# A speech joint's backward pass: the rows of two gradients taken by transposing DMAs, from sets written in a row by VectorE

## The chip, the cores and the metric

The kernel runs on one core of a Trainium2 chip. The metric is the device time of one execution in microseconds; before, three runs gave a median of 848.4 us (845.08 to 851.57). The profile is of one execution that took 843.12 us.

## What is computed

A sequence `x` of 2 x 16000 frames of 256 goes through two convolutions of three taps with a tanh-approximated gelu and a stride of 2 after each (16000 to 8000 to 4000 frames). The result `f` (projected to `fe`) is joined with 8 label vectors `ge`, and the kernel returns the joint's output and the gradients of all seven inputs for a given `grad_out`. All in bfloat16.

```python
def _fwd_reference(x, w1, w2, g, w_f, w_g, w_o):
    ...
    h = _gelu(h)[:, ::2, :]          # h: conv of x with w1, 3 taps
    ...
    f = _gelu(f)[:, ::2, :]          # f: conv of h with w2, 3 taps
    fe = jnp.einsum("btd,de->bte", f, w_f)
    ge = jnp.einsum("bud,de->bue", g, w_g)
    j = jnp.tanh(fe[:, :, None, :] + ge[:, None, :, :])
    return jnp.einsum("btud,dv->btuv", j, w_o)

def reference(x, w1, w2, g, w_f, w_g, w_o, grad_out):
    ...
    _out, _vjp = jax.vjp(_f, x, w1, w2, g, w_f, w_g, w_o)
    return (_out, *_vjp(grad_out))
```

## The kernel before, in words

Time is counted in quarter frames (one column of the kernel is one frame of `f`, four of `x`). The 2 x 4000 columns with a gap of 16 between them are cut into 16 stages of 512 columns (the last has 336; stage 7 holds the end of one batch and the start of the next, and its transfers are split). Channels lie on the partitions, 256 of them as two halves (`kt`), and time runs along the free axis.

In the loop over stages `n`, stage `n` does the joint of its own columns, the forward convolutions of stage `n+1`, and the backward of stage `n-1` below the joint. It has four steps (`up`), each for two of the eight labels. The joint is the main list, 12 units a step: the products with `WOT` (L623), the tanh gradient `NGZ` on VectorE (L627), its sum over the labels on GpSimd (L646, the last of which writes `NGFE`, bf16), the output's products (L690), their eviction on ScalarE (L692), and the gradient of `w_o` (L729). `weave` takes after each main unit 0.92 units on the average of a second list, the fill, which is a chain written out by hand:

- `conv` of stage `n+1` (L320) and `d1` (L424, the gradient through `w_f`, makes `GF`);
- `alternate(rows, d5)`: `row_units` turns `NGFE`, and the sets of `HT` and `GF`, into rows (time on the partitions) by TensorE transposes (L460), evicted by VectorE (`NGFE`) or ScalarE (L462); `d5_units` (L447) multiplies with `W2T` and VectorE writes the product with the gelu's derivative as `GH` (L450), the gradient at the first convolution's output, for even and odd frames (`par` 0 and 1);
- `gwf_units` (L506, gradient of `w_f`, from `FR` and the rows of `NGFE`) and `gw2_units` (L524, gradient of `w2`);
- `ghr_units`: the rows of `GH`, in four interleaved sets (columns k, k+4, k+8, ...), by 16 transposes on TensorE and two evictions on VectorE; between them `conv2` of stage `n+1` (L355);
- `e_units`: blocks of the gradient of `x` (L580, from `GH`), each evicted (L583) and stored by GpSimd (L241), and after each of the first three blocks one tap of the gradient of `w1` (`gw1`, L593, from the rows of `GH` and of `x`). `fe` of stage `n+1` (L379) lies among them.

Operations of an engine run in the order in which they are issued. SyncE's queue takes all transposing loads and the `grad_out` rows: `GOT` (L172, `grad_out` with channels on partitions), `XC` (L164, `x` of stage `n+2`, one a step at the end of each step in the program), `GO` (L198), `FR` (L469, rows of `f`, read in the next stage) and `JR` (L658, rows of the tanh). GpSimd's queue takes the rows of `x` (`XR`, L209) and the stores. In a regular stage SyncE issues: JR JR GOT GO XC GOT XC XC XC JR JR GOT GO GOT FR FR JR JR GO GOT GOT JR JR GO GOT GOT.

Of the kernel before, what the change touches and what calls it, by code (L numbers as in the profile page):

```python
# [13 lines left out]
BF16 = mybir.dt.bfloat16  # L14
# [18 lines left out]
def kernel(  # L33
# [76 lines left out]
    accp = pool("accp", 1)  # L110
    gfp = pool("gfp", 2)
    ghp = pool("ghp", 2)
    rowp = pool("rowp", 6)
    xrp = pool("xrp", 1)
    gxp = pool("gxp", 2)
    jtp = pool("jtp", 7)
# [313 lines left out]
    def d5_units(n):  # L430
        st = S[n]
        c0, W = geom(n)
        N = W + 1 if n == G - 1 else W
        GF, G1 = st["GF"], st["G1"]
        GH = ghp.tile([P, 2, KT, CW + 4], BF16, name="GH")
        st["GH"] = GH
        if n == 0:
            nc.gpsimd.memset(GH[:, 0, :, 1:2], 0.0)
        else:
            nc.gpsimd.tensor_copy(out=GH[:, 0, :, 1:2], in_=S[n - 1]["GH"][:, 0, :, CW + 1:CW + 2])  # L440
        for par, taps in ((0, ((1, 0),)), (1, ((2, -1), (0, 0)))):
            for mt in range(KT):
                ps = ps_f32()
                k, last = 0, len(taps) * KT - 1
                for (i, sh) in taps:
                    for kt in range(KT):
                        nc.tensor.matmul(ps[:, :N], lhsT=W2T[:, i, kt, mt * P:(mt + 1) * P],  # L447
                                         rhs=GF[:, kt, 2 + sh:2 + sh + N], start=(k == 0), stop=(k == last))
                        k += 1
                gh = nc.vector.tensor_tensor(out=GH[:, par, mt, 2:2 + N], in0=ps[:, :N],  # L450
                                             in1=G1[:, par, mt, 2 - par:2 - par + N], op=ALU.mult)
                while held:
                    tc.add_manual_dep(held.pop().ins, gh.ins.name, NOSYNC, reason="held")
                yield

    def transposes(srcs, dsts, evict=None):
# [4 lines left out]
        for dst, M, j0, j1 in dsts:  # L461
            (evict or nc.vector.tensor_copy)(out=dst, in_=ps[:M, j0:j1, :])  # L462

    def load_fr(n):
        W = geom(n)[1]
        FR = frp.tile([P, KT, 4, P], BF16, name="FR")
        nb = len(blocks(W))
        for kt in range(KT):
            nc.sync.dma_start_transpose(out=FR[:, kt, 0:nb, :], in_=S[n]["FT"][:, kt, 0:nb * P])  # L469
        S[n]["FR"] = FR  # L470

    def row_units(n):
        c0, W = geom(n)
        st = S[n]
        HT, GF, FT, NG = st["HT"], st["GF"], st["FT"], st["NGFE"]
        bl = blocks(W)
        FR = st["FR"]
        t = rowp.tile([P, 8, P], BF16, name="rows")
        st["NR"] = t
        srcs = [(NG[:, kt, o:o + M], 2 * j + kt, M) for j, (o, M) in enumerate(bl) for kt in range(KT)]  # L480
        dsts = [(t[:M, 2 * j:2 * j + 2, :], M, 2 * j, 2 * j + 2) for j, (o, M) in enumerate(bl)]
        if W == CW:
            dsts = [(t[:], P, 0, 8)]
        transposes(srcs, dsts)
        yield
# [12 lines left out]

    def gwf_units(n):
        W = geom(n)[1]  # L500
        FR, t = S[n]["FR"], S[n]["NR"]
        bl = blocks(W)
        ps = ps_f32()
        for k, (o, M) in enumerate(bl):
            for dt in range(KT):
                nc.tensor.matmul(ps[:, dt * D:(dt + 1) * D], lhsT=FR[:M, dt, k, :],  # L506
                                 rhs=t[:M, 2 * k:2 * k + 2, :].rearrange("p k d -> p (k d)"),
                                 start=(k == 0 and dt == 0), stop=(k == len(bl) - 1 and dt == KT - 1))
        flush("F", ACCF[:], ps[:])
        first_flush["F"] = False  # L510
        yield
# [27 lines left out]
    def back_sets(n):  # L539

        return [(k, M + 1 if n == G - 1 and k == 0 else M) for k, M in sets(n)]

    def ghr_units(n):
        st = S[n]
        s = nsets(n)
        GH = st["GH"]
        bl = back_sets(n)
        GR = st["GR"] = []
        for g0 in range(0, len(bl), 2):
            t = rowp.tile([P, 8, P], BF16, name="rows")  # L550
            srcs, dsts = [], []
            for j, (k, M) in enumerate(bl[g0:g0 + 2]):
                for par in range(2):
                    for kt in range(KT):
                        srcs.append((GH[:, par, kt, 2 + k:3 + k + s * (M - 1):s], 4 * j + 2 * par + kt, M))
                dsts.append((t[:M, 4 * j:4 * j + 4, :], M, 4 * j, 4 * j + 4))
                GR.append((t, 4 * j))
            if all(M == P for _, M in bl[g0:g0 + 2]):
                dsts = [(t[:, :, :], P, 0, 8)]
            transposes(srcs, dsts)  # L560
            yield

    def e_units(n):
        st = S[n]
        s = nsets(n)
        GH, GR, XR = st["GH"], st["GR"], st["XR"]
        bl = back_sets(n)

        def gx_block(k, M):
            t = gxp.tile([P, 4, D], BF16, name="GX")  # L570
            combos = (((0, 1, 0), (2, 0, -1)), ((1, 1, 0),), ((2, 1, 0), (0, 0, 0)), ((1, 0, 0),))
            for cp in range(2):
                ps = ps_f32()
                for cj in range(2):
                    cc = combos[2 * cp + cj]
                    j, last = 0, len(cc) * KT - 1
                    for (i, par, sh) in cc:
                        for kt in range(KT):
                            o = 2 + k + sh
                            nc.tensor.matmul(ps[:M, cj * D:(cj + 1) * D], lhsT=GH[:, par, kt, o:o + s * (M - 1) + 1:s],  # L580
                                             rhs=W1T[:, i, kt, :], start=(j == 0), stop=(j == last))
                            j += 1
                nc.scalar.copy(out=t[:M, 2 * cp:2 * cp + 2, :], in_=ps[:M, :])  # L583
                yield
            store_gx(n, k, t)

        def gw1(i):
            ps = ps_f32()
            for j, (k, M) in enumerate(bl):
                t, g = GR[j]  # L590
                for dt in range(KT):
                    for par in range(2):
                        nc.tensor.matmul(ps[:, dt * D:(dt + 1) * D],  # L593
                                         lhsT=XR[:M, 4 * k + i + 2 * (1 - par), dt * P:(dt + 1) * P],
                                         rhs=t[:M, g + 2 * par:g + 2 * par + 2, :].rearrange("p k d -> p (k d)"),
                                         start=(j == 0 and dt == 0 and par == 0),
                                         stop=(j == len(bl) - 1 and dt == KT - 1 and par == 1))
            flush("1", ACC1[:, i, :], ps[:])
# [225 lines left out]
    for n in range(G):  # L824
# [75 lines left out]
    for b in range(B):  # L900
        gg = ps_f32()
        for kt in range(KT):
            nc.tensor.matmul(gg[:U, 0:D], lhsT=NGGEb[:, b, kt, :], rhs=WGT[:, kt, :], start=(kt == 0), stop=(kt == KT - 1))
        gg_sb = gxp.tile([U, D], BF16, name="gg_sb")
        nc.scalar.activation(out=gg_sb[:], in_=gg[:U, 0:D], func=ACT.Copy, scale=-1.0)
        nc.sync.dma_start(out=out_4[b], in_=gg_sb[:])
# [3 lines left out]
        ngR = gxp.tile([U, KT, P], BF16, name="ngR")  # L910
        nc.vector.tensor_copy(out=ngR[:], in_=tr[:U, 0:KT, :])
# [37 lines left out]
```

## Time and profile before

| | |
|---|---|
| median of three runs | 848.4 us (845.08 to 851.57) |
| the profiled execution | 843.12 us |
| its span in the profile | 841.4 us |
| mean granted TensorE clock | 0.994 |
| mean DMA traffic | 187.21 MB, 223 GB/s |
| length of a stage | 50.7 to 51.2 us, 53.0 for stage 8 |

The first part of the page gives each engine's busy time, its share of the span and the instructions; the second cuts the span in 40 slices, each digit the busy share in tenths. The groups give, for a line and its tiles, the count, then the busy time and the mean ns of one, then the idle time ahead of them and what ended it. In a timeline, columns are the start, the length, the engine, the line and the tiles, and the number of instructions; of SyncE's queue (SPq) the length is the time that the issue took, not the transfer.

Some more rows: how the pieces of the queue land, from issue to landing, as the page's medians.

```profile
GOT<-in_grad_out_dram SPq DMA_TRANSPOSE x136, 5.7
JR<-JT SPq DMA_TRANSPOSE x128, 4.8
```

### The profile page before, as it was taken

How to read it: one execution, taken by the hardware profiler on the slowest of the kernel's cores; microseconds unless marked ns; L12 is line 12 of the kernel's file. 1: busy time of each engine (PE TensorE's matmuls, PEld its weight loads, DVE VectorE, ACT ScalarE, POOL GpSimd, SP SyncE). 2: the span in 40 equal slices, each digit the busy share in tenths (PEclk: the TensorE clock that was granted, in tenths of full speed). 3: DMA queues.
4: the chain of work that ended last, by engine and by line, in shares of the span. 5: the costliest groups of instructions: out<-in, count | busy, mean ns of one | idle time of the engine just before them, and what ended most of it. 6: DMA issues, size and time to landing. Idle time of an engine off the chain costs nothing.

```text
span 841.4 us, 17055 instructions
## 1 busy us (share of the span) xinstructions
PE 812.8 (97%) x6396; PEld 598.2 (71%) x6396; DVE 620.3 (74%) x1217; ACT 678.4 (81%) x1080; POOL 394.6 (47%) x423
## 2 busy tenths in 40 slices
PE   7969999999999999999999999999999999999997
PEld 3546677767768677676766777677686776878796
DVE  4896696876778767697866968768687676967644
ACT  3889998796978969699796987969789696987744
POOL 1154544444534535444486644445345354445661
PEclk9999999999999999999999999999999999999999
DMA  9988999999999999999999999999999999999954
GB/s 188 194 198 182 212 229 233 216 251 235 225 221 259 226 229 245 243 222 183 224 255 210 233 233 228 251 210 265 238 237 264 210 227 231 220 210 228 243 157 135
DMA packets 398515, 187.21 MB, mean 223 GB/s; under 512 B 346464, under 2 KB 382200, under 8 KB 398432
## 3 DMA queue, kind: packets, MB, share of 16 engines
q1 hardware_dynamic: 378112, 119.00, 77.9%
q0 software_dynamic: 20320, 67.12, 27.5%
q8 instruction: 50, 0.82, 0.4%
q14 instruction: 33, 0.27, 0.1%
HBM read 51.38 MB, written 50.34 MB: 121 GB/s over the span
## 4 chain that ended last, share of the span: by engine, by line
PE 43%; ACT 41%; DVE 6%; issue 5%; DMA 4%; POOL 0%; SPq 0%; ACTq 0%; POOLq 0%; DVEq 0%
ACT JT L396 12%; PE ps L593 7%; ACT OUT L692 6%; ACT JSQ L617 6%; PE GWO_ps L729 6%; PE ps L580 6%; PE ps L690 6%; ACT rows L462 5%; PE ps L355 5%; PE ps L524 4%; PE ps L623 4%; ACT g_s L260 3%; ACT g_x L323 3%; PE pst L460 2%; ACT GX L583 2%
## 5 line engine op out<-in xcount | busy, mean ns | idle before, releaser
L646 POOL TENSOR_TENSOR ACCN<-ACCN,NGZ 128x1024 f32<-128x1024 f32 (+1 forms) x80 | 168.7, 2109 | 69.1 <-DVE NGZ L627 68.0
L627 DVE SCALAR_TENSOR_TENSOR NGZ<-JSQ,ps 128x512 bf16<-128x512 bf16 (+3 forms) x272 | 167.5, 640 | 43.2 <-PE ps L623 39.9
L692 ACT CAST OUT<-ps 128x512 bf16<-128x512 f32 (+1 forms) x252 | 148.4, 600 | 58.4 <-PE ps L690 58.2
L396 ACT ACTIVATE JT<-FE,GE 128x512 bf16<-128x512 f32 (+3 forms) x272 | 182.3, 711 | 4.0 <-PE ps L623 1.9
L617 ACT ACTIVATE JSQ<-JT 128x1024 bf16<-128x1024 bf16 (+1 forms) x128 | 135.8, 1064 | 25.6 <-DVE NGZ L627 25.6
L729 PE MATMUL GWO_ps<-GO,JR 128*128 128x256 bf16 (+1 forms) x1008 | 148.6, 273 | 2.1 <-DVE JR L462 2.1
L690 PE MATMUL ps<-WO,JT 128*128 128x256 bf16 (+1 forms) x1008 | 148.7, 274 | 0.3 <-ACT rows L462 0.3
L717 POOL DMA_DIRECT2D out_dram<-OUT x76 | 55.8, 735 | 184.4 <-ACT OUT L692 171.5
L623 PE MATMUL ps<-GOT,WOT 128*128 128x512 bf16 (+1 forms) x512 | 139.2, 376 | 0.8 <-DVE rows L462 0.8
L260 DVE SCALAR_TENSOR_TENSOR g_s<-g_sq,g_x 128x1024 bf16<-128x1024 bf16 (+2 forms) x49 | 81.2, 1657 | 50.1 <-ACT g_sq L260 50.1
L729 PEld LDWEIGHTS <-JR 128*128 128x128 bf16 (+1 forms) x1008 | 96.9, 98 | 28.6 <-DVE JR L462 2.4
L690 PEld LDWEIGHTS <-JT 128*128 128x128 bf16 (+1 forms) x1008 | 97.9, 98 | 22.1 <-issue 1.6
L580 PE MATMUL ps<-W1T,GH 128*128 128x256 bf16 (+2 forms) x756 | 100.4, 273 | 0.0
L408 DVE TENSOR_TENSOR ACC<-ACC,ps 128x512 f32<-128x512 f32 x90 | 61.5, 684 | 44.5 <-PE ps L524 32.8
L580 PEld LDWEIGHTS <-GH 128*128 128x128 bf16 (+2 forms) x756 | 83.5, 116 | 13.0
L320 PE MATMUL ps<-XC,W 128*128 128x512 bf16 (+1 forms) x384 | 91.3, 375 | 1.1 <-DMA XC<-in_x_dram 1.1
L593 PE MATMUL ps<-rows,XR 128*128 128x256 bf16 (+1 forms) x756 | 90.4, 273 | 0.0
L593 PEld LDWEIGHTS <-XR 128*128 128x128 bf16 (+1 forms) x756 | 74.0, 98 | 11.6
L583 ACT CAST GX<-ps 128x512 bf16<-128x512 f32 (+2 forms) x126 | 72.2, 587 | 10.5 <-DMA out_dram<-GX 4.1
L241 POOL DMA_DIRECT2D out_dram<-GX x67 | 36.7, 548 | 82.1 <-ACT GX L583 75.0
L623 PEld LDWEIGHTS <-WOT 128*128 128x128 bf16 x512 | 48.5, 98 | 33.6 <-issue 2.3
L320 PEld LDWEIGHTS <-W 128*128 128x128 bf16 x384 | 37.4, 98 | 38.5 <-issue 1.4
(131 smaller groups left out, 1214.2 us busy)
## 6 DMA issues: line engine op xcount, KB each, us to landing
GO<-in_grad_out_dram SPq DMA_DIRECT2D x56, 512.0 KB, 5.3
out_dram<-OUT POOLq DMA_DIRECT2D x56, 512.0 KB, 5.5
out_dram<-GX POOLq DMA_DIRECT2D x55, 256.0 KB, 4.3
XR<-in_x_dram POOLq DMA_DIRECT2D x39, 256.0 KB, 6.3
XR<-in_x_dram POOLq DMA_DIRECT2D x13, 320.0 KB, 6.2
GOT<-in_grad_out_dram SPq DMA_TRANSPOSE x136, 5.7
JR<-JT SPq DMA_TRANSPOSE x128, 4.8
GO<-in_grad_out_dram SPq DMA_DIRECT2D x4, 384.0 KB, 5.0
```

The lines of the kernel that those rows point to most:

```text
L260: later.popleft()()
L320: nc.tensor.matmul(ps[:, :W], lhsT=W1[:, i, kt, mt * P:(mt + 1) * P], rhs=st["X", c][:, kt, 16 + sh:16 + sh + W], start=(k == 0), stop=(k ...
L396: nc.scalar.activation(out=JT[:, mt, lo:hi], in_=S[n]["FE"][:, mt, lo:hi], func=ACT.Tanh, bias=GE[:, b, mt, u:u + 1], scale=1.0)
L580: nc.tensor.matmul(ps[:M, cj * D:(cj + 1) * D], lhsT=GH[:, par, kt, o:o + s * (M - 1) + 1:s], rhs=W1T[:, i, kt, :], start=(j == 0), stop=( ...
L593: nc.tensor.matmul(ps[:, dt * D:(dt + 1) * D], lhsT=XR[:M, 4 * k + i + 2 * (1 - par), dt * P:(dt + 1) * P], rhs=t[:M, g + 2 * par:g + 2 * ...
L617: nc.scalar.activation(out=JSQ[:, :, :W], in_=JT[:, :, :W], func=ACT.Square)
L623: nc.tensor.matmul(ps[:, :W], lhsT=WOT[:, kt, mt * P:(mt + 1) * P], rhs=GOT[:, kt, :W], start=(kt == 0), stop=(kt == KT - 1))
L627: nc.vector.scalar_tensor_tensor(out=NGZ[:, mt, lo:hi], in0=JSQ[:, mt, lo:hi], scalar=1.0, in1=ps[:, lo:hi], op0=ALU.subtract, op1=ALU.mul ...
L646: st["last"] = nc.gpsimd.tensor_tensor(out=out, in0=in0, in1=st["NGZ", u][:, :, :W], op=ALU.add)
L690: nc.tensor.matmul(ps[:M, j * V:(j + 1) * V], lhsT=st["JT", u][:, kt, o:o + M], rhs=WO[:, kt, :], start=(kt == 0), stop=(kt == KT - 1))
L692: nc.scalar.copy(out=OUT[:M, k, :], in_=ps[:M, :])
L729: nc.tensor.matmul(GWO_ps[:, dt, :], lhsT=JR[:M, j, dt, k, :], rhs=GO[:M, k, j * V:(j + 1) * V], start=(n_gwo[0] == 0), stop=(n_gwo[0] == ...
```

## The change

The rows of `NGFE` (now `NR`) and of `GH` (now `GR`) come from transposing DMAs on SyncE's queue in all stages but the last; the transposes and evictions for them are gone there (the last stage keeps them).

- `GH` is split in two tiles, `GH0` and `GH1` (for the two `par`). VectorE writes each as four sets of 128 one after the other (the sets in reverse), reading the product in PSUM and the gelu's derivative `G1` at a step of four elements, so that a set is contiguous and one DMA turns 128-column blocks of it. The weights read from `GH` for the gradient of `x` are contiguous then.
- `load_gr` issues for each stage `GR0` as two halves (by `kt`) and `GR1` as one DMA, in the place of the fill where the rows and `d5` are done; they take no fill unit. `load_nr` issues `NR` of stage `n-1` at the start of stage `n`. `FR` becomes one DMA in place of two.
- In SyncE's queue a regular stage becomes: NR JR JR GOT GO GOT XC XC XC XC GR0 JR JR GOT GO GR0 GOT GR1 FR JR JR GO GOT GOT JR JR GO GOT GOT.
- The list of the fill: `ghr` before `gwf` and `gw2`, without the two units that it had; `rows` has one unit less (the `NGFE` rows).
- Pools: `rowp` has 4 buffers in place of 6, `NR` one and `GR` two of their own. Two small tiles of the tail move to `rowp`.

```diff
-    rowp = pool("rowp", 6)
+    rowp = pool("rowp", 4)
+    nrp = pool("nrp", 1)
+    grp = pool("grp", 2)
...
+        turned = n < G - 1
+        GH0 = ghp.tile([P, KT, CW + 4], BF16, name="GH0")
+        GH1 = ghp.tile([P, KT, CW], BF16, name="GH1")
+        st["GH"] = GH = (GH0[:, :, 2:CW + 4], GH1)
+        st["GHB"] = GH0[:, :, 1:CW + 4]
...
-                gh = nc.vector.tensor_tensor(out=GH[:, par, mt, 2:2 + N], in0=ps[:, :N],
-                                             in1=G1[:, par, mt, 2 - par:2 - par + N], op=ALU.mult)
+                out, in0, in1 = GH[par][:, mt, :N], ps[:, :N], G1[:, par, mt, 2 - par:2 - par + N]
+                if turned:
+                    out = out.rearrange("p (k m) -> p k m", k=4)
+                    in0, in1 = (bass.AP(tensor=a.tensor, offset=a.offset + 3, ap=[list(a.ap[0]), [-1, 4], [4, P]]) for a in (in0, in1))
+                gh = nc.vector.tensor_tensor(out=out, in0=in0, in1=in1, op=ALU.mult)
...
+    def load_rows(pool_, name, src, W):
+        t = pool_.tile([P, KT, 4, P], BF16, name=name)
+        if W == CW:
+            nc.sync.dma_start_transpose(out=t[:].rearrange("p k a d -> p (k a) d"), in_=src.rearrange("p k w -> p (k w)"))
+        else:
+            nb = len(blocks(W))
+            for kt in range(KT):
+                nc.sync.dma_start_transpose(out=t[:, kt, 0:nb, :], in_=src[:, kt, 0:nb * P])
+        return t
...
     def load_fr(n):
-        for kt in range(KT):
-            nc.sync.dma_start_transpose(out=FR[:, kt, 0:nb, :], in_=S[n]["FT"][:, kt, 0:nb * P])
-        S[n]["FR"] = FR
+        S[n]["FR"] = load_rows(frp, "FR", S[n]["FT"][:], geom(n)[1])
+
+    def load_nr(n):
+        S[n]["NR"] = load_rows(nrp, "NR", S[n]["NGFE"][:], geom(n)[1])
...
+    def load_gr(src, par):
+        if par:
+            return load_rows(grp, "GR", src[:], CW)
+        t = grp.tile([P, KT, 4, P], BF16, name="GR")
+        for kt in range(KT):
+            nc.sync.dma_start_transpose(out=t[:, kt], in_=src[:, kt, :CW])
+        return t
...
+        if n < G - 1:
+            ts = [load_gr(GH[par], par) for par in range(2)]
+            GR += [[t[:, :, 3 - k, :] for t in ts] for k in range(4)]
+            return
...
             parts += [islice(conv, 2), islice(d1, 1), islice(conv, 1), d1, conv, alternate(rows, d5_units(n - 1)),
-                      gwf_units(n - 1), gw2_units(n - 1), islice(ghr, 1), islice(conv2, 1), ghr, conv2, islice(e, 6)]
+                      ghr, gwf_units(n - 1), gw2_units(n - 1), conv2, islice(e, 6)]
...
+            if back and up == 0:
+                load_nr(n - 1)
```

More of the change, by code (lines that the diff above doesn't have):

```diff
@@ L434, in d5_units @@
         GF, G1 = st["GF"], st["G1"]
-        GH = ghp.tile([P, 2, KT, CW + 4], BF16, name="GH")
-        st["GH"] = GH
+        turned = n < G - 1
[3 more added lines that the diff above has]
+        st["GHB"] = GH0[:, :, 1:CW + 4]
         if n == 0:
-            nc.gpsimd.memset(GH[:, 0, :, 1:2], 0.0)
+            nc.gpsimd.memset(GH0[:, :, 1:2], 0.0)
         else:
-            nc.gpsimd.tensor_copy(out=GH[:, 0, :, 1:2], in_=S[n - 1]["GH"][:, 0, :, CW + 1:CW + 2])
+            nc.gpsimd.tensor_copy(out=GH0[:, :, 1:2], in_=S[n - 1]["GHB"][:, :, P:P + 1])
         for par, taps in ((0, ((1, 0),)), (1, ((2, -1), (0, 0)))):
@@ L462, in transposes @@
             (evict or nc.vector.tensor_copy)(out=dst, in_=ps[:M, j0:j1, :])
-    def load_fr(n):
-        W = geom(n)[1]
-        FR = frp.tile([P, KT, 4, P], BF16, name="FR")
-        nb = len(blocks(W))
-        for kt in range(KT):
-            nc.sync.dma_start_transpose(out=FR[:, kt, 0:nb, :], in_=S[n]["FT"][:, kt, 0:nb * P])
-        S[n]["FR"] = FR
+    def load_rows(pool_, name, src, W):
[7 more added lines that the diff above has]
+        return t
+    def load_fr(n):
+        S[n]["FR"] = load_rows(frp, "FR", S[n]["FT"][:], geom(n)[1])
+    def load_nr(n):
+        S[n]["NR"] = load_rows(nrp, "NR", S[n]["NGFE"][:], geom(n)[1])
     def row_units(n):
@@ L477, in row_units @@
         FR = st["FR"]
[L478 to L485, printed above, removed]
+        if "NR" not in st:
+            t = nrp.tile([P, KT, 4, P], BF16, name="NR")
+            st["NR"] = t
+            ps = ps_bf()
+            for j, (o, M) in enumerate(bl):
+                for kt in range(KT):
+                    nc.tensor.transpose(out=ps[:M, 4 * kt + j, :], in_=NG[:, kt, o:o + M], identity=ident[:])
+            for j, (o, M) in enumerate(bl):
+                nc.vector.tensor_copy(out=t[:M, :, j, :], in_=ps[:M, j:j + 5:4, :])
+            yield
         st["HG"] = []
@@ L506, in gwf_units @@
                 nc.tensor.matmul(ps[:, dt * D:(dt + 1) * D], lhsT=FR[:M, dt, k, :],
-                                 rhs=t[:M, 2 * k:2 * k + 2, :].rearrange("p k d -> p (k d)"),
+                                 rhs=t[:M, :, k, :],
                                  start=(k == 0 and dt == 0), stop=(k == len(bl) - 1 and dt == KT - 1))
@@ L541, in back_sets @@
         return [(k, M + 1 if n == G - 1 and k == 0 else M) for k, M in sets(n)]
+    def load_gr(src, par):
+        if par:
+            return load_rows(grp, "GR", src[:], CW)
+        t = grp.tile([P, KT, 4, P], BF16, name="GR")
+        for kt in range(KT):
+            nc.sync.dma_start_transpose(out=t[:, kt], in_=src[:, kt, :CW])
+        return t
     def ghr_units(n):
@@ L548, in ghr_units @@
         GR = st["GR"] = []
+        if n < G - 1:
+            ts = [load_gr(GH[par], par) for par in range(2)]
+            GR += [[t[:, :, 3 - k, :] for t in ts] for k in range(4)]
+            return
         for g0 in range(0, len(bl), 2):
-            t = rowp.tile([P, 8, P], BF16, name="rows")
+            t = grp.tile([P, KT, 4, P], BF16, name="GR")[:].rearrange("p k a d -> p (k a) d")
             srcs, dsts = [], []
@@ L554, in ghr_units @@
                     for kt in range(KT):
-                        srcs.append((GH[:, par, kt, 2 + k:3 + k + s * (M - 1):s], 4 * j + 2 * par + kt, M))
+                        srcs.append((GH[par][:, kt, k:k + s * (M - 1) + 1:s], 4 * j + 2 * par + kt, M))
                 dsts.append((t[:M, 4 * j:4 * j + 4, :], M, 4 * j, 4 * j + 4))
-                GR.append((t, 4 * j))
+                GR.append([t[:M, 4 * j + 2 * par:4 * j + 2 * par + 2, :] for par in range(2)])
             if all(M == P for _, M in bl[g0:g0 + 2]):
@@ L565, in e_units @@
         s = nsets(n)
-        GH, GR, XR = st["GH"], st["GR"], st["XR"]
+        GH, GHB, GR, XR = st["GH"], st["GHB"], st["GR"], st["XR"]
         bl = back_sets(n)
@@ L578, in gx_block @@
                         for kt in range(KT):
-                            o = 2 + k + sh
-                            nc.tensor.matmul(ps[:M, cj * D:(cj + 1) * D], lhsT=GH[:, par, kt, o:o + s * (M - 1) + 1:s],
+                            if k + sh < 0:
+                                gh = GHB[:, kt, 0:s * (M - 1) + 1:s] if n == G - 1 else GHB[:, kt, 0:M]
+                            elif n == G - 1:
+                                gh = GH[par][:, kt, k + sh:k + sh + s * (M - 1) + 1:s]
+                            else:
+                                gh = GH[par][:, kt, (3 - k - sh) * P:(3 - k - sh) * P + M]
+                            nc.tensor.matmul(ps[:M, cj * D:(cj + 1) * D], lhsT=gh,
                                              rhs=W1T[:, i, kt, :], start=(j == 0), stop=(j == last))
@@ L589, in gw1 @@
             for j, (k, M) in enumerate(bl):
-                t, g = GR[j]
                 for dt in range(KT):
@@ L594, in gw1 @@
                                          lhsT=XR[:M, 4 * k + i + 2 * (1 - par), dt * P:(dt + 1) * P],
-                                         rhs=t[:M, g + 2 * par:g + 2 * par + 2, :].rearrange("p k d -> p (k d)"),
+                                         rhs=GR[j][par],
                                          start=(j == 0 and dt == 0 and par == 0),
@@ L903 @@
             nc.tensor.matmul(gg[:U, 0:D], lhsT=NGGEb[:, b, kt, :], rhs=WGT[:, kt, :], start=(kt == 0), stop=(kt == KT - 1))
-        gg_sb = gxp.tile([U, D], BF16, name="gg_sb")
-        nc.scalar.activation(out=gg_sb[:], in_=gg[:U, 0:D], func=ACT.Copy, scale=-1.0)
-        nc.sync.dma_start(out=out_4[b], in_=gg_sb[:])
+        gg_sb = rowp.tile([P, 8, P], BF16, name="rows")[:U, 0:2, :].rearrange("u a b -> u (a b)")
+        nc.scalar.activation(out=gg_sb, in_=gg[:U, 0:D], func=ACT.Copy, scale=-1.0)
+        nc.sync.dma_start(out=out_4[b], in_=gg_sb)
         tr = ps_bf()
@@ L909 @@
             nc.tensor.transpose(out=tr[:U, kt, :], in_=NGGEb[:, b, kt, :], identity=ident[:])
-        ngR = gxp.tile([U, KT, P], BF16, name="ngR")
-        nc.vector.tensor_copy(out=ngR[:], in_=tr[:U, 0:KT, :])
+        ngR = rowp.tile([P, 8, P], BF16, name="rows")[:U, 0:KT, :]
+        nc.vector.tensor_copy(out=ngR, in_=tr[:U, 0:KT, :])
         for dt in range(KT):
```

## The prediction

> **What bounds the kernel now.** I read the busy shares first, then the slices, the queues, and for one regular stage TensorE beside SyncE's queue.
>
> ```profile
> PE 812.8 (97%) x6396; PEld 598.2 (71%) x6396; DVE 620.3 (74%) x1217; ACT 678.4 (81%) x1080; POOL 394.6 (47%) x423
> PE   7969999999999999999999999999999999999997
> DMA  9988999999999999999999999999999999999954
> q1 hardware_dynamic: 378112, 119.00, 77.9%
> q0 software_dynamic: 20320, 67.12, 27.5%
> ```
>
> TensorE is busy 97% of the span and sets the end; the chain of waits ends in its products or in their ACT evictions. But the DMA row is as full: q1 carries what SyncE issues, 119 MB, nearly all transposes in small packets; q0 what GpSimd issues. So there are two resources at their end, and the change moves work from the one to the other.
>
> The work to be removed, in the groups of instructions by form:
>
> ```profile
> L450 DVE TENSOR_TENSOR GH<-ps,G 128x512 bf16<-128x512 f32 x60 | 40.2, 684 | 2.4 <-PE ps L447 2.2
> L462 DVE COPY rows<-pst 128x1024 bf16<-128x1024 bf16 x45 | 31.0, 688 | 29.0 <-PE pst L460 29.0
> L460 PE MATMUL pst<-ident,GH 128*128 128x128 bf16 x240 | 18.3, 219 | 0.0
> L460 PE MATMUL pst<-ident,NGFE 128*128 128x128 bf16 x124 | 9.5, 219 | 0.0
> ```
>
> TensorE in stage 3 (start 172.3, counted from the stage's first L623 product), its first read of the GH rows being the L593 line, +32.5 us:
>
> ```profile
> 197.39 0.61 PE L460 MATMUL pst<-ident,GH 128*128 128x128 bf16 x8
> ...
> 199.58 0.61 PE L460 MATMUL pst<-ident,GH 128*128 128x128 bf16 x8
> ...
> 204.80 1.91 PE L593 MATMUL ps<-rows,XR 128*128 128x256 bf16 x16
> ```
>
> SyncE's queue in the same stage:
>
> ```profile
> 172.57 3.23 SPq L658 DMA_TRANSPOSE JR<-JT  x2
> 175.90 2.99 SPq L172 DMA_TRANSPOSE GOT<-in_grad_out_dram  x1
> 178.94 0.57 SPq L198 DMA_DIRECT2D GO<-in_grad_out_dram  x1
> 179.61 3.70 SPq L164 DMA_TRANSPOSE XC<-in_x_dram  x1
> 183.40 1.86 SPq L172 DMA_TRANSPOSE GOT<-in_grad_out_dram  x1
> 185.35 6.20 SPq L164 DMA_TRANSPOSE XC<-in_x_dram  x3
> 191.66 4.89 SPq L658 DMA_TRANSPOSE JR<-JT  x2
> 196.64 1.28 SPq L172 DMA_TRANSPOSE GOT<-in_grad_out_dram  x1
> 197.97 0.57 SPq L198 DMA_DIRECT2D GO<-in_grad_out_dram  x1
> 198.64 1.95 SPq L172 DMA_TRANSPOSE GOT<-in_grad_out_dram  x1
> 200.69 3.37 SPq L469 DMA_TRANSPOSE FR<-FT  x2
> ```
>
> From 172.6 to 204.1 there is no gap in this queue. Each transfer starts when the one before has been issued, not when its data are ready: FR, whose source is long written, starts at +28.4. This is the row that decides: the GR loads are queued right ahead of it.
>
> **The change part by part.** All sums are against the profiled execution, 843.1 us (span 841.4 and 1.7 around it), which is 5.3 under the median 848.4; the times move with it.
>
> 1. Removed from TensorE: 8 NGFE and 16 GH transposes in a stage, 15 stages. Eight in a row take 0.61 us with the last at 0.219, so one is (0.61 - 0.219)/7 = 0.056 us and a stage's 24 are 1.34 us, 20.1 us in all. TensorE being full, this is gain if nothing else is late: a stage of 50.8 us would take some 49.3.
>
> 2. Removed from DVE: three evictions in a stage, 3 x 0.688 = 2.06 us. DVE is 74% busy and off the path; nothing by itself.
>
> 3. GH read at a step of four and written in a row. No row has this read. Bounds: nothing, and the 1657 ns for 1024 columns of DVE's gelu products, 1.62 ns a column where L450 has 684/512 = 1.34, that is 829 ns, +0.15 us, four times a stage 0.6 us. I take 0.6: DVE has 2.06 us to spare from part 2, and GH is finished at +19.6, long before SyncE's queue comes to it. Cover gone, 0.6 us a stage.
>
> 4. FR by one DMA in place of two halves: the issue mean of JR, the same shape, is 1.73 us, two halves at the FR median of 1.42 are 2.84. 1.1 us less on the queue, but behind the GR loads, so GR has nothing of it. The gx weight loads from GH become contiguous (114 to 98 ns); weight loads overlap products, nothing. The gg_sb and ngR buffers are in the tail and short: nothing.
>
> 5. Added on SyncE: NR, at the head of the stage; GR0 in two halves; GR1. In the new order ten DMAs go before GR0's first half, GR1 is the 18th of the stage, and FR, two JR, GO and two GOT follow it. The NR issue waits for the summed gradient NGFE, which POOL finishes at +0.2, and holds all of the queue until then; in stage 3 the queue's first DMA started at +0.27 anyhow: nothing, up to 0.3. NR is read by gwf (L506 at 191.1, +18.8), lands at about +0.2 + 4.8, so it has ten us and more to spare. The first gw1 product, which waited for a DVE eviction, waits for GR1's landing instead.
>
> 6. When GR1 lands. FR began in stages 1 to 13 between 24.7 (stage 1, with nothing carried over) and 37.2 (stage 7, which holds the end of one batch and the start of the next, and has split transfers). Without stages 7 to 10, which carry that along, the median is 28.0. A stage that waits lets the queue drain, so I take 26.5, between 24.7 and 28.0. Ahead come NR (1.73, the JR mean) and GR0 (two halves, 2 x 1.42): +4.6. Issue to landing 4.8, the JR median on the page (FR's whole has 5.6). GR1 lands at 26.5 + 4.6 + 4.8 = +35.9. Bounds: 24.7 + 3.6 + 3.6 = 31.9 and 28.4 + 5.2 + 7.2 = 40.8, with three issues at 1.2 us (the FR minimum) or at JR's mean, and landings of 3.6 and 7.2, the ends of what FR took in stages 1 to 5.
>
> 7. When gw1 wants it. GH rows lie three fill units and their transposes earlier in the list of before; with those gone, the products that stand ahead of the first L593 sum to 2.2 us less than in before, so it comes at 32.5 - 2.2 = +30.3; I take +30.0. The wait is 35.9 - 30.0 = 5.9 us (bounds 1.9 and 10.8). TensorE takes its work in order, so the joint's products queue behind it, then ACT and DVE, and nothing covers it. What follows gw1 in the stage is 19.1 us of products, so the stage is 35.9 + 19.1 = 55.0 us.
>
> 8. A wait of that size also lowers TensorE's clock. In before it happens once, in stage 0 after three gaps between 52.4 and 62.0 of 1.6, 2.1 and 1.5 us:
>
> ```profile
> 57.00:60.40 3.40, 1.27 (x11) 0.84 (x10) 3.40 (x4) 2.56 (x5) 3.32 (x2) 1.00 0.48 154
> 60.40:67.20 6.80, 5.32 (x18) 2.46 (x17) 4.69 (x8) 4.68 (x8) 1.38 (x2) 0.50 0.24 80
> ```
>
> (columns: stretch, its length, PE, PEld, DVE, ACT, POOL busy with counts, granted clock, DMA share, GB/s). 6.8 us at a clock of 0.50 lose 3.4 us at the most; DVE and ACT were busy 4.7 of 6.8, so I take 0.69 x 3.4 = 2.3 (bounds 0 and 3.4). The Trainium skill, "TensorE: Matmul & The Clock Gate", Part 1 (the HAM clock gate), says that an idle window of about 3.4 us halves the clock and a busy one of that length restores it; by that rule the loss is 1.7 us a stage after every wait over 3.4 us, and the row above, with 6.8 us at half clock, asks for more.
>
> Sum: 55.0 + 2.3 - 50.8 = +6.5 us in each of stages 1 to 13, 85 us. Stages 14 and 15 have no XC transfers in front (four, 2.08 us each), so GR1 is there in time and they save 1.3 us each, 2.7. 843.1 + 85 - 3 = **925 us**.
>
> **The rivals.**
>
> *GR1 is there in time (faster).* The removed 20.1 us are all gained: 843 - 20 = 823 us. For it: the data are ready at +19.6, GR has 10 us. It decides if the 17 DMAs ahead take under 25 us, that is if the queue's issues are near their least (1.2 us) and not at their means of 1.4 to 2.1; against it, FR in no stage began before +24.7, and the DMA engines, whose row is full, get 768 KB a stage more. Chance 0.08.
>
> *Only the rate of the queue binds.* If waits adapt (the stage's length is what SyncE needs for its list), the price is three more issues a stage. Before, the backlog of stage 7 is worked off by about 1.6 us a stage, so the list needs 49.2; with 3 x 1.2 to 3 x 1.63 it is 52.8 to 54.1, TensorE's waits being shorter than 3.4 us and the clock full. (52.8 - 50.8) x 13 - 3 = +23, or +40: 866 to 883 us. For it: the waits make the queue start each stage early. Against it: NR at the head holds the queue until the stage's start, so that it can't run ahead. Chance 0.14.
>
> *Longer waits, at half clock.* GR1 at its late bound and the loss at 3.4: 40.8 + 19.1 + 3.4 - 50.8 = 12.5 a stage, 843 + 163 - 3 = 1003; from 985 on. For it: stages 7 to 10 with FR at +33 to +37. Against: those carried a backlog. Chance 0.07.
>
> *It does what it says, and nothing shows:* the gain of 1.3 us and a wait of the same size, 843 +- 8; a landing at +31.3 would do it, and nothing in the rows aims there. Chance 0.03.
>
> **How the numbers follow.** The likeliest, a wait for GR1 in every regular stage, has 0.68 and gives 925, between 880 and 985. With the rate case (0.14) the range goes down to 866; left out are the faster case, no change, the long waits, 0.18 in all. Range 866 to 985. About 1% is what a measurement of this kernel can tell from no change: faster 0.08, same 0.03, slower 0.89.
>
> **What would show it.** In the profile after: L593 products idle before them on a DMA of GR, 4 to 9 us in each regular stage and nearly nothing in stages 14 and 15; a stage of 55 to 59 us; the granted clock at half behind the waits; TensorE's share down to some 87%; GR1's issue at +31 and landing at +36, FR behind it; L450 at 684 to 830 ns; NR landed before +8 with no one waiting for it. I am wrong if the L593 wait is short while the time is up (then the queue's rate, or JR and GOT behind GR1, is what binds), if GR1 is issued before +26, or if DVE's GH products come out so slow that they, and not the queue, hold GR back.

## The result and the profile after

The changed kernel takes 1008.1 us (median; 1001.5 to 1018.0), the kernel before, run beside it, 846.7: a ratio of 1.188 (95% interval 1.177 to 1.198). It is slower, by twice what was forecast and above the forecast's range. The profiled execution took 1005.8 us, its span is 1004.1.

The busy shares and slices of the page, after:

```profile
PE 821.7 (82%) x5959; PEld 584.3 (58%) x6036; DVE 565.4 (56%) x1172; ACT 685.2 (68%) x1080; POOL 398.7 (40%) x423
PE   8979696978949799695896967959799497978768
PEclk9989798998979989798897997979999798998979
DMA  9969899898997979999699897998989989797964
q1 hardware_dynamic: 425632, 130.80, 71.3%
```

TensorE's row, a row of nines before, has a dip about once a stage, and the clock dips with it. The DMA row has dips as well: nothing is full any more. q1 moves 11.8 MB more, 45 times 256 KB. The groups by form, and TensorE's waits:

```profile
L459 DVE TENSOR_TENSOR GH<-ps,G 128x512 bf16<-128x512 f32 x60 | 40.1, 685 | 11.5 <-PE ps L452 10.7 <-PE ps L724 0.6
L627 PE MATMUL ps<-GR,XR 128*128 128x256 bf16 x720 | 112.4, 318 | 153.6 <-DMA GR<-GH 98.5 <-issue 51.3 <-ACT JSQ L651 3.7
```

VectorE reads at a step of four in 685 ns where it took 684: that part is free. The idle time of 153.6 us ahead of gw1 (L627 now) is nearly all of the 163 us that the span grew by. ("issue" there is the same wait in stages where the trace names no releaser: in every stage from 1 to 14 the gap ahead of the first gw1 product begins at +24 to +28 and lasts 3.7 to 13.4 us; in stage 15 it is 7.8 us ahead of the second.) Times with a plus count from the start of the stage. Stage 3, which starts at 192.65, on TensorE:

```profile
218.52 1.03 PE L657 MATMUL ps<-GOT,WOT 128*128 128x512 bf16 x4
228.31 0.37 PE L627 MATMUL ps<-GR,XR 128*128 128x256 bf16 x1 [8.76 <-DMA GR<-GH]
230.01 3.36 PE L627 MATMUL ps<-GR,XR 128*128 128x256 bf16 x15 [1.33 <-DMA GR<-GH]
```

and on SyncE's queue:

```profile
203.07 11.79 SPq L166 DMA_TRANSPOSE XC<-in_x_dram  x4
214.96 1.22 SPq L566 DMA_TRANSPOSE GR<-GH  x1
216.28 3.52 SPq L692 DMA_TRANSPOSE JR<-JT  x2
219.89 2.15 SPq L174 DMA_TRANSPOSE GOT<-in_grad_out_dram  x1
222.09 0.59 SPq L200 DMA_DIRECT2D GO<-in_grad_out_dram  x1
222.77 1.23 SPq L566 DMA_TRANSPOSE GR<-GH  x1
224.09 2.31 SPq L174 DMA_TRANSPOSE GOT<-in_grad_out_dram  x1
226.49 1.44 SPq L475 DMA_TRANSPOSE GR<-GH  x1
...
233.08 3.50 SPq L174 DMA_TRANSPOSE GOT<-in_grad_out_dram  x2
245.13 3.79 SPq L692 DMA_TRANSPOSE JR<-JT  x2
```

TensorE is ready for gw1 at 219.55 (228.31 - 8.76), +26.9. The first product reads GR0, whose second half is issued at 222.77, the second product reads GR1, issued at 226.49, +33.8; it runs at 230.01, +37.4. The two waits are 10.1 us. `GH` was complete at +17.0; GR1 stood for 17 us behind XC, JR and GOT. The last two lines show what the wait does to the queue: from 236.6 to 245.1 SyncE issues nothing. The queue's own waits over the run (us in total, times, the longest) name the reason:

```profile
SPq L692 <- PE GWO_ps L763: 116.3, 14, 8.6
```

There are two buffers for JR. The next JR is written over one that products of the gradient of `w_o` (L763) still read, and these stand behind gw1 on TensorE; in stage 3 the last of them ends at 245.07. Every stage from 1 to 14 has such a gap ahead of JR, of 7.4 to 8.6 us. So the wait for GR holds back the queue in its turn, and the loss isn't made up later in the stage.

The granted clock over the wait (columns as before: stretch, length, PE, PEld, DVE, ACT, POOL, clock, DMA share, GB/s):

```profile
222.00:226.00 4.00, 0.00 (x0) 0.00 (x0) 0.06 (x1) 0.55 (x1) 2.04 (x1) 0.72 0.96 197
226.00:230.00 4.00, 0.37 (x1) 0.14 (x2) 0.00 (x0) 0.00 (x0) 0.00 (x0) 0.50 1.29 253
230.00:234.00 4.00, 3.79 (x16) 2.54 (x17) 0.59 (x1) 0.00 (x0) 0.00 (x0) 0.50 0.99 176
234.00:238.00 4.00, 4.00 (x35) 3.40 (x35) 3.96 (x10) 2.62 (x4) 1.15 (x2) 1.00 1.28 218
```

VectorE, ScalarE and GpSimd stand still with TensorE; the first tap of gw1 runs at half clock. The profiled execution of the version "XC behind" below fell in a slower state of the chip, so the table has no stage figures for it.

### The profile page after: what moved, and what is told of

Read it like the earlier page. It is cut to its first block, busy times and chain, and to the rows that moved or that the text cites. A ratio compares the mean times of both kernels' runs of the same rounds, so it can differ in the third digit from the quotient of the medians.

```text
span 1004.1 us, 16305 instructions
## 1 busy us (share of the span) xinstructions
PE 821.7 (82%) x5959; PEld 584.3 (58%) x6036; DVE 565.4 (56%) x1172; ACT 685.2 (68%) x1080; POOL 398.7 (40%) x423
## 4 chain that ended last, share of the span: by engine, by line
PE 64%; ACT 11%; DMA 8%; DVE 8%; SPq 6%; issue 3%; POOL 0%; ACTq 0%; POOLq 0%; DVEq 0%
PE ps L627 10%; PE ps L724 9%; PE GWO_ps L763 8%; PE ps L657 7%; PE ps L615 6%; PE ps L322 6%; DMA GR<-GH 6%; PE ps L542 4%; PE ps L357 3%; PE ps L452 3%; SPq L174 3%; DVE g_s L262 3%; ACT JT L398 2%; PE pst L468 2%; ACT g_sq L262 2%
## 5 line engine op out<-in xcount | busy, mean ns | idle before, releaser
L627 PE MATMUL ps<-GR,XR 128*128 128x256 bf16 (+1 forms) x756 | 116.9, 316 | 153.6 <-DMA GR<-GH 98.5
L680 POOL TENSOR_TENSOR ACCN<-ACCN,NGZ 128x1024 f32<-128x1024 f32 (+1 forms) x80 | 174.6, 2182 | 43.6 <-DVE NGZ L661 41.5
L627 PEld LDWEIGHTS <-XR 128*128 128x128 bf16 (+1 forms) x756 | 83.3, 111 | 182.2 <-issue 163.9
L726 ACT CAST OUT<-ps 128x512 bf16<-128x512 f32 (+1 forms) x252 | 146.0, 603 | 55.3 <-PE ps L724 55.2
L398 ACT ACTIVATE JT<-FE,GE 128x512 bf16<-128x512 f32 (+3 forms) x272 | 176.2, 714 | 9.4 <-DMA JR<-JT 9.0
L410 DVE TENSOR_TENSOR ACC<-ACC,ps 128x512 f32<-128x512 f32 x90 | 61.7, 686 | 210.7 <-PE ps L627 189.6
L763 PE MATMUL GWO_ps<-GO,JR 128*128 128x256 bf16 (+1 forms) x1008 | 149.1, 273 | 6.5 <-DMA JR<-JT 3.6
L657 PE MATMUL ps<-GOT,WOT 128*128 128x512 bf16 (+1 forms) x469 | 130.9, 382 | 1.2 <-ACT rows L470 0.3
L763 PEld LDWEIGHTS <-JR 128*128 128x128 bf16 (+1 forms) x1008 | 97.8, 98 | 38.3 <-DMA JR<-JT 3.8
L262 DVE SCALAR_TENSOR_TENSOR g_s<-g_sq,g_x 128x1024 bf16<-128x1024 bf16 (+2 forms) x49 | 63.0, 1285 | 97.7 <-ACT g_sq L262 97.5
L724 PEld LDWEIGHTS <-JT 128*128 128x128 bf16 (+1 forms) x1008 | 99.0, 99 | 26.9 <-issue 2.6
L615 PEld LDWEIGHTS <-GH 128*128 128x128 bf16 (+2 forms) x756 | 76.7, 104 | 18.9 <-issue 5.2
L322 PEld LDWEIGHTS <-W 128*128 128x128 bf16 x384 | 37.4, 98 | 38.1 <-issue 1.0
```

The costliest lines, as they stand in the source:

```text
L262: later.popleft()()
L322: nc.tensor.matmul(ps[:, :W], lhsT=W1[:, i, kt, mt * P:(mt + 1) * P], rhs=st["X", c][:, kt, 16 + sh:16 + sh + W], start=(k == 0), stop=(k ...
L398: nc.scalar.activation(out=JT[:, mt, lo:hi], in_=S[n]["FE"][:, mt, lo:hi], func=ACT.Tanh, bias=GE[:, b, mt, u:u + 1], scale=1.0)
L615: nc.tensor.matmul(ps[:M, cj * D:(cj + 1) * D], lhsT=gh, rhs=W1T[:, i, kt, :], start=(j == 0), stop=(j == last))
L627: nc.tensor.matmul(ps[:, dt * D:(dt + 1) * D], lhsT=XR[:M, 4 * k + i + 2 * (1 - par), dt * P:(dt + 1) * P], rhs=GR[j][par], start=(j == 0 ...
L657: nc.tensor.matmul(ps[:, :W], lhsT=WOT[:, kt, mt * P:(mt + 1) * P], rhs=GOT[:, kt, :W], start=(kt == 0), stop=(kt == KT - 1))
```

## The experiments

Two theories. **Place**: the queue has room, but GR stands too far back in it and its reader too far forward in TensorE's list. **Rate**: three more transposes of 256 KB a stage are more than SyncE's queue and the DMA engines carry in a stage of 51 us, wherever they stand. A third question was what the half clock costs. The stage lengths below are means over stages 2 to 13, from the end of one `NGFE` sum to the next; the DMA share and the clock are the rows of those windows; "SyncE idle" is the sum of the gaps of more than 0.2 us between issues in a stage, without those ahead of NR, where SyncE waits for the end of the `NGFE` sum.

| kernel | us (median) | ratio, interval | stage | DMA share | clock | SyncE idle |
|---|---|---|---|---|---|---|
| before | 844.7 to 846.7 | | 51.0 | 1.11 | 1.00 | 1.1 |
| changed | 1008.1 | 1.188 (1.177 to 1.198) | 61.7 | 0.97 | 0.91 | 9.7 |
| gw1 last | 920.1 | 1.083 (1.069 to 1.097) | 55.7 | 1.11 | 0.96 | 0.3 |
| gw1 last, XC behind | 908.4 | 1.070 (1.060 to 1.080) | 55.3 | 1.12 | 0.98 | 0.2 |
| gw1 last, no GX stores | 893.6 | 1.056 (1.048 to 1.063) | 53.8 | 1.10 | 0.98 | 0.2 |
| XC behind | 930.9 | 1.098 (1.088 to 1.108) | | | | |
| 30 dummy products | 1007.5 | 1.192 (1.182 to 1.202) | 61.7 | 0.98 | 0.96 | 9.1 |
| 42 dummy products | 1006.0 | 1.189 (1.179 to 1.200) | 60.8 | 0.99 | 0.99 | 8.4 |
| GR alone | 941.1 | 1.116 (1.110 to 1.122) | 59.1 | 1.01 | 0.93 | 7.0 |
| NR alone | 874.2 | 1.033 (1.025 to 1.040) | 53.2 | 1.12 | 0.99 | 0.1 |
| NR alone, not turned | 857.1 | 1.012 (1.004 to 1.019) | 51.4 | 1.12 | 0.99 | 0.2 |
| sets, no new DMA | 845.7 | 1.001 (0.998 to 1.003) | 51.1 | 1.12 | 1.00 | 0.6 |
| before, no GX stores | 840.0 | 0.994 (0.992 to 0.996) | 50.8 | 1.08 | 1.00 | 2.5 |
| before, FR by TensorE | 857.8 | 1.015 (1.013 to 1.018) | 52.1 | 1.11 | 1.00 | 2.1 |

**The reader later.**

```diff
             yield from gx_block(k, M)
-            if j < KK:
-                gw1(j)
-                yield
+        for j in range(KK):
+            gw1(j)
+            yield
```

> The changed kernel with the three gw1 taps moved behind the blocks of the gradient of x in the fill; nothing else is touched, the queue keeps its DMAs and their order. Theory P (place): in the changed kernel TensorE waits because GR1 lands at about +37 (18th in the queue) and its reader stands at +27; the queue itself has room (8.6 us idle in stage 3). The reader now comes at about +38, so waits are 0 to 4 us, the stage is 49 to 51 us and the time 825 to 855 us plus what the last two stages still lose, up to 20. Theory R (rate): three more transposes a stage are more than SyncE's queue and the DMA engines can carry in 50 us; a stage stays at 53 us or more and TensorE waits for JR, GOT or XC in place of GR: 880 us or more.

920 us: 88 us of the 162 are gone, but not the rest. It lies between the theories. TensorE's waits now:

```profile
PE ps L627 <- DMA GR<-GH: 43.6, 16, 5.0
PE GWO_ps L763 <- DMA JR<-JT: 17.7, 18, 2.7
```

and the slices:

```profile
PE   8989799896997979979599998989989899799877
DMA  9969999999999999999999999999999999999882
```

The dips of the DMA row are gone, SyncE issues nearly without a gap (0.3 us idle a stage, 9.7 in the changed kernel), and still the stage is 55.7 us. That points to the rate. It isn't the rate alone yet: GR still lands late in some stages, and in stages 3 to 5 SyncE waits 1.5 to 3.1 us ahead of NR (0.8 us a stage in the mean).

**The loads earlier.** XC loads ordered behind GR1 on SyncE's queue.

```diff
+                if n >= 3 and "grd" in S[n - 3]:
+                    tc.add_manual_dep(dma.ins, S[n - 3]["grd"].ins.name, NOSYNC, reason="x behind the rows")
```

> The changed kernel with three of the four XC loads of a stage queued behind GR1. Theory P: GR1 is the 15th and the three XC issues of 8.9 us in stage 3 are no longer ahead; it lands at about +29, the wait at gw1 is about 2 us (too short for half clock), the stage 50 to 52 us, the time 850 to 885 us with what stages 14 and 15 lose, where no XC is left to move. Theory R: the transfers are only swapped, the wait goes to another tile and the time stays above 940 us.

931 us, again between the two: place is worth 77 us from this side. Three of the four XC loads were to move; in the queue of the run all four of a regular stage stand behind GR1, which becomes the 14th transfer of the stage.

**Both.**

> gw1 last in the fill and three XC loads behind GR1, both at once. Theory R (rate): with gw1 last SyncE's queue ran without a gap (0.1 to 0.5 us idle a stage) at 55.7 us a stage, so the rate is the floor; the waits of TensorE for GR (43.6 us) go to XC, JR or GOT instead and the time is 900 to 925 us. Theory P (place): without the waits for GR the stage is 52 us and the time 860 to 880 us.

908 us, as the rate theory had it. The waits for GR fall from 43.6 to 7.2 us, and the time goes to the rows of the tanh on the same queue instead:

```profile
PE GWO_ps L768 <- DMA JR<-JT: 29.3, 23, 3.0
ACT JT L400 <- DMA JR<-JT: 68.9, 26, 8.2
```

TensorE waits for JR to land. ScalarE waits for the same loads (1.6 us in the kernel before), since it can write the next tanh only into a buffer that JR's transfer has read. So with the place put right at both ends a loss of some 62 us stays, with a queue that has 0.2 us idle a stage.

**One transfer alone.** The kernel before, with only NGFE's rows by a DMA (`load_nr` as in the change; `FR` in two halves).

> The kernel before with only the rows of NGFE by a DMA at the head of the stage; the GH rows stay on TensorE, GH is written as before, FR stays in two halves. One transpose more a stage on the queue, 8 of TensorE's less and one fill unit less. Theory P: nothing waits on NR, which lands at about +7; the gain is 8 x 0.056 x 15 = 6.7 us, 836 to 842 against 846.7. Theory R: the queue was full with 49.2 us a stage, one more is 50.4 to 50.8, and the time stays within 5 us of before or is above it, with JR's landing close to its use.

874 us: the place theory missed by over 30 us, and the 50.4 to 50.8 us a stage of the rate theory are 53.2. No wait for NR stands in the trace. TensorE waits again for the tanh rows behind it, and less for `GF` from VectorE:

```profile
PE GWO_ps L745 <- DMA JR<-JT: 20.5, 15, 3.0
PE pst L461 <- DVE GF L427: 5.8, 6, 2.8
```

SyncE's idle time goes from 1.1 to 0.1 us and the stage from 51.0 to 53.2. A kernel whose queue was nearly without slack paid 28 us for one transfer a stage that nothing waits for.

**The same transfer, not turned.**

```diff
-        S[n]["NR"] = load_rows(nrp, "NR", S[n]["NGFE"][:], geom(n)[1])
+        t = S[n]["NR"] = nrp.tile([P, KT, 4, P], BF16, name="NR")
+        nc.sync.dma_start(out=t[:].rearrange("p k a d -> p k (a d)"), in_=S[n]["NGFE"][:])
```

> The kernel with the rows of NGFE alone by DMA, but the DMA copies NGFE as it lies (2 KB a partition) and does not turn it, so the gradient of w_f comes out of wrong rows; the count of DMAs, their place and their bytes are as before that edit. If the price of NR (28 us, some 2 us a stage) is the transposing transfer's 1024 small packets, it goes away: 836 to 848 us. If it is the place at the head of SyncE's queue (JR waits behind it until NGFE is done), it stays at 865 to 876.

857 us, between the two: 17 of the 28 us go with the turning, at the same bytes and the same place. The issue of NR on SyncE takes, at the least, in the middle and at the most (ns), plain and turned:

```profile
L477 SPq DMA_DIRECT2D NR<-NGFE x15: 475/542/579, 72.1 to 785.3; - x15
L468 SPq DMA_TRANSPOSE NR<-NGFE x15: 1231/2522/4838, 69.9 to 805.5; - x15
```

The 2.0 us between the middles are close to the 1.8 us by which the stages differ (53.2 and 51.4). Whether it is this issue time or the packets on the DMA engines (1056 a transfer turned, 144 plain, by q1's count), the run can't tell: both go together.

Of the other 11 us (interval of the ratio 1.004 to 1.019) the profile shows 10.4, and 6.5 of them lie in stage 15 and the tail. There a step has four JR transfers, and NR stands ahead of the first four:

```profile
798.46 1.04 ACT L397 ACTIVATE JT<-FE,GE 128x336 bf16<-128x336 f32 x2 [6.52 <-DMA JR<-JT]
800.23 1.01 PE L707 MATMUL ps<-WO,JT 128*128 128x256 bf16 x4 [5.49 <-ACT rows L463]
```

ScalarE waits until JR's transfers have read a tanh buffer that it is to write, and TensorE waits for the row evictions that stand behind this on ScalarE. The kernel before has no such wait on TensorE there (0.3 us); NR alone, turned, has both (6.8 and 5.8 us). The second JR is issued only 0.5 us later than before, at +1.9, but lands at +13.1 in place of +7.5. So it isn't the place at the head that costs there, but that the queue's transfers land later; why they do was not tested.

**Fewer bytes elsewhere.** The stores of the gradient of x left out in stages 1 to 14, so most of that output isn't written; on top of gw1 last, and on the kernel before.

> gw1 last in the fill, and the stores of the gradient of x left out in all stages but the first and the last (so most of that output is not written): about 1 MB less a stage on the GpSimd queue, nothing changed on SyncE's queue. If the DMA engines are the bound, 1 MB at the 230 GB/s of a stage is 4.4 us, and the stage goes from 55.7 to about 51.3 us: 860 us. If SyncE's issuing is the bound by itself (28 issues at their least), the time stays at 910 to 925.

> The kernel before with the stores of the gradient of x left out in all stages but the first and the last (most of that output is not written), as was done to the changed kernel with gw1 last, where it took 26 us off. If the kernel before is bound by TensorE alone, which waits for 1.2 us a stage, the time stays within 5 us of before. If it is held by the DMA engines as well, by the same 1.9 us a stage, it falls towards what TensorE's 49.8 us of work a stage allow, 825 to 835.

With the new transfers it gives 26 us (920.1 to 893.6), under half of the 60 expected; without them 0.6%, 5 us. So GpSimd's stores do take from SyncE's transfers where these bind, though much less than bytes over GB/s. The kernel before was bound by TensorE: without the stores it is idle for 1.0 us a stage, with them for 0.9.

**The opposite step.** `load_fr` gone, FR by 8 transposes and an eviction in `row_units`.

> The opposite step: the kernel before with the rows of f (FR) turned by TensorE too, 8 transposes and one VectorE eviction of 0.69 us more a stage, two half DMAs less. If the DMA engines hold the kernel before (51 us a stage at a full share), they need 1.5 us less, TensorE 0.45 us more (49.8 + 0.45), and the time falls by up to 10 us, to 835 to 845. If TensorE alone is the bound, it rises by 0.45 x 16 = 7 us, 850 to 858.

858 us, 13 more, at the upper end of what TensorE as the bound was to give, though its sum had 7. The other half is a wait: the products of the gradient of `w2` wait more for ScalarE's row evictions, over stages 2 to 13, here and before:

```profile
PE ps L535 <- ACT rows L462: 11.5, 23, 0.8
PE ps L524 <- ACT rows L462: 4.4, 11, 0.4
```

That is 0.6 of the 1.1 us by which a stage grew. TensorE bound the kernel before, and taking a transfer away gains nothing; the eviction took 683 ns as forecast. Note the DMA share: 1.11 in a kernel that has two half transfers fewer a stage and isn't bound by them. So the share of time that packets take doesn't tell whether the DMA engines bind. SyncE's idle time does better here: 0.1 to 0.3 us a stage in the versions held by the queue (NR alone, gw1 last and its two variants), 0.6 to 2.5 in those held by TensorE. NR not turned, 11 us slower than before, has 0.2.

**The layout alone.** The changed kernel with all rows but FR from TensorE at their old places in the fill; VectorE evicts the `NGFE` rows in four pieces in place of one.

```diff
-            ts = [load_gr(GH[par], par) for par in range(2)]
-            GR += [[t[:, :, 3 - k, :] for t in ts] for k in range(4)]
-            return
+            for g0 in range(0, len(bl), 2):
...
+                            srcs.append((GH[par][:, kt, (3 - k) * P:(4 - k) * P], 4 * j + 2 * par + kt, M))
...
-            if back and up == 0:
-                load_nr(n - 1)
...
-                      ghr, gwf_units(n - 1), gw2_units(n - 1), conv2, islice(e, 6)]
+                      gwf_units(n - 1), gw2_units(n - 1), islice(ghr, 1), islice(conv2, 1), ghr, conv2, islice(e, 6)]
```

> The changed kernel without its new DMAs: GH is read at a step and written in sets, FR is one DMA, and the rows of GH and NGFE come from TensorE transposes at the places in the fill that they had before. If all of the loss is in the DMAs (rate and place), this is the time before, 838 to 850 us, and DVE's GH products take 684 ns as before. If the new layout costs by itself, 855 or more.

845.7 us, a ratio of 1.001: the sets, the read at a step and the single FR transfer neither cost nor gain together, and all of the loss is in NR's and GR's DMAs and the new order of the fill that comes with them.

```profile
L459 DVE TENSOR_TENSOR GH<-ps,G 128x512 bf16<-128x512 f32 x60 | 40.2, 686 | 2.3 <-PE ps L452 2.2
```

**GR alone by DMA.** `load_nr` left out of the changed kernel, NGFE's rows by TensorE.

> The changed kernel with the rows of NGFE by TensorE; only GH's rows by DMA. Rate alone: two transposes more at 1.5 us a stage, 54 us, 890. Place and rate: GR1 is issued 1.7 us earlier than in the changed kernel, at about +32.3, lands at +36, its reader stands at +28, and the stage is 36 + 21 + 2 = 59 us: 950 to 975.

941 us, a little under the 950 to 975 of place and rate together, whose sum of 59 us a stage came (59.1). Its stages 1 and 13 are also a test of the clock. In stage 13 TensorE waited 1.66 us, the first tap ran its other 15 products in 1.80 us, which is full clock, and the stage was 51.5 us:

```profile
806.75 0.27 PE L627 MATMUL ps<-GR,XR 128*128 128x256 bf16 x1
808.68 1.80 PE L627 MATMUL ps<-GR,XR 128*128 128x256 bf16 x15 [1.66 <-DMA GR<-GH]
```

In stages 2 to 12 the waits are longer, and it is 6.2 to 7.2 us from the tap's second product to the next tap's first, where stages 1 and 13 take 4.2.

**The clock.** 30 and then 42 products whose result nothing reads, ahead of the first tap.

```diff
+            if i == 0 and 1 <= n < G - 1:
+                pw = ps_f32()
+                for _ in range(30):
+                    tc.keep_in_program_order(nc.tensor.matmul(pw[:], lhsT=W1[:, 0, 0, 0:P], rhs=W1[:, 0].rearrange("p k d -> p (k d)"),
+                                                              start=True, stop=True))
```

> The changed kernel with 30 products of 512 columns, whose result is read by nothing, ahead of the first gw1 tap of each stage: 6.5 us of work in a wait of about 10 us. If the half clock behind the wait costs what the rows show (some 16 products of 256 columns at 0.213 in place of 0.109 us and two more, 2.2 us a stage), the time falls by about 30 us to 978; if other engines hide it, the time stays at 1008; if the waits are shorter than 6.5 us, the time rises.

> As the run with 30 dummy products, but 42 of them, 9.1 us of a wait of about 10 to 11 us. With 30 the rest of the wait was 4 us in most stages and the clock still fell there; only stages 2, 10 and 12 kept it, and the first tap took 4.2 us in place of 5.6 to 7.0. If the half clock costs, the taps take about 4.2 us in most stages now, 2.3 us less, and the time falls by 20 to 35 us to 975 to 990; if the loss is taken up elsewhere, the time stays within 1% of 1008 though the clock is up.

1007.5 and 1006.0: the clock rose from 0.91 to 0.96 and 0.99, the time did not move by more than its scatter. With 30, the rest of the wait was still enough to lower the clock; stage 3 there:

```profile
223.50 0.27 PE L632 MATMUL ps<-GR,XR 128*128 128x256 bf16 x1 [2.46 <-DMA GR<-GH]
225.29 3.36 PE L632 MATMUL ps<-GR,XR 128*128 128x256 bf16 x15 [1.52 <-DMA GR<-GH]
```

Two stages lie close to the border: gaps of 0.75 and 1.88 us kept the clock (30 dummies, stage 10), gaps of 1.04 and 1.94 us lost it (42 dummies, stage 10).

With 42 the span from the tap's second product to the next tap fell from 6.3 to 4.8 us in the mean, but the second product came 0.5 us later, since in stages where GR landed early (11, 12, 13: +33 to +36) the dummies themselves held TensorE to +35.9. In the profile the net is 0.9 us a stage; in the medians nothing can be told. What the half clock costs the whole is therefore open between nothing and about 2 us a stage. One thing came out clean: in stages 3, 11, 12 and 13, where TensorE had no wait left at gw1, the stage took 57.6 us, of which 42 x 0.2158 = 9.1 are dummies. The rest, 48.5 us, is an estimate of TensorE's own work in a stage of the changed kernel.

## Why the prediction was wrong

The sign, the place of the wait (gw1's first tap, on GR, in every regular stage) and its mechanism came as forecast. The size did not: 1008 against 925; in stage 3 the wait was 10.1 us against 5.9. The step that failed is part 7, when the reader comes; the landing in part 6 and the sum's last term, stages 14 and 15, were also off. By the prediction's own steps:

- **Parts 1 and 2, TensorE's and VectorE's work**: right; 48.5 us of work a stage against the forecast 49.3. None of the gain reaches the end of the stage, since it lies ahead of the wait.
- **Part 3, the read at a step**: taken at 0.6 us a stage, it costs nothing (685 ns, and 1.001 for the layout alone).
- **Part 5, NR**: nobody waits for it, as said. But it was priced at nothing, and alone it costs 28 us, most of it through the queue behind it. That a transfer with time to spare is free was wrong in a queue without idle time.
- **Part 6, GR1's landing**: forecast +35.9; its reader's second product ran at +37.8 in the mean of stages 2 to 13, issued at +34.0 and not +31.1, and landing in 3.8 us and not 4.8. A miss of 1.9 us, inside the bounds. (The median of FR's begins, given as 28.0, is 28.4 in the rows; the 26.5 taken is below both.)
- **Part 7, the reader**: this is the step that failed in the regular stages. "The products that stand ahead of the first L593 sum to 2.2 us less" put gw1 at +30.0; in stage 3 TensorE stood at it at +26.9, and GH's last write comes at +17.0 in place of +19.5 in most stages. Three fill units fewer ahead of gw1 bring forward not only their own work. The weave puts about one unit of the joint between two units of the fill, and so 8 products on GOT (1.7 us) and 4 on JT (0.4) moved behind gw1 too; one block of `conv`, 6 products (1.3 us), is issued before the stage's start; and the gaps of 0.8 us for the transposes are gone. 3.1 us earlier is 3.1 us more of wait, and more work left behind it: 23.9 us from the second product to the stage's end against 19.1 + 2.3. Per stage 37.8 + 23.9 = 61.7 us against 57.3: of the 4.4 us missed, 2.5 are this step's and 1.9 part 6's.
- **Part 8, the half clock**: the size was right, 6.3 in place of 4.2 us for the first tap. That all of it lies on the path was not shown. By the Trainium skill, "TensorE: Matmul & The Clock Gate", Part 1 (the HAM clock gate), an idle window of about 3.4 us halves the clock; the 1.66 us wait that kept it and the 8.76 us wait that lost it agree, and so do the two gaps of 2.46 and 1.52 with one product between them, if they count as one; those of 1.04 and 1.94 lost the clock with 3.25 us in all, product included, a little under that figure.
- **Stages 14 and 15**: forecast to save 2.7 us, they and the tail cost 22 (14: 55.1 against 47.7; 15 and tail: 74.5 against 60.0). The sum took away the XC loads and forgot the rest. In stage 14 TensorE waits 6.6 us for the second half of GR0 and 1.1 for GR1, in stage 15 7.8 us for GR1, which is issued at +28.3 and +29.8. Stage 15's columns need four JR transfers a step instead of two, eight of them ahead of GR1, and its shorter products bring the reader to +25.5.

Stages 1 to 13 give 803.1 - 661.3 = 142 us of the loss, where 85 were forecast: of the 57 missed, about 32 are part 7's and 25 part 6's. Stages 14 and 15 with the tail missed another 25. Of the rivals, *longer waits* (1003 us, given 0.07) is where the time came out, but not as it was put there: GR1 landed well inside its bounds, at +37.8 and not +40.8, and the reader came earlier. That the time met this rival's was luck. *Only the rate binds* was the floor under the whole: its 52.8 to 54.1 us a stage were 55.3 when place was put right. It priced an added issue at 1.2 to 1.63 us; NR alone took 2.5 us to issue, in a queue without idle time. The 49.2 us that it started from are near what the kernel before shows (51.0 less 1.1 idle).

No version here with a new transfer beats the kernel before: the layout alone equals it, and the new transposing transfers, NR alone and GR alone as well as both, cost more than the transposes that they replace.

## What to carry to other kernels

When work moves from a full engine to a full queue, price it twice: by the rate (is there any idle time in that queue's issues at all?) and by the place (what stands ahead of it, and when its reader comes). Work out when the reader comes from the whole new order of the reading engine; a unit taken from one of two woven lists pulls the other list's units out from in front of it as well. A transfer that lands long before its use is not free where the queue behind it has readers with less slack.

## What had not been expected of the hardware

- Reading PSUM (float32) and SBUF (bf16) at a step of four elements cost VectorE nothing: 685 against 684 ns for 128x512.
- One SBUF to SBUF transposing transfer of 256 KB a stage costs this kernel 2.2 us of a stage; the same bytes copied plainly 0.4 (53.2 and 51.4 against 51.0, stages 2 to 13).
- No kernel here had a DMA share above 1.12 over stages 2 to 13, bound by its DMAs or not.
